# A transformer block on one core: a second annealed instruction order, from a model with another cost for GpSimd's power

## The chip, the cores and the metric

The kernel runs on one core of one Trainium2 chip. Times are device microseconds of one execution. Each kernel ran several times, in turns with the kernel before on the same chip. A few executions have a slightly lower granted TensorE clock (a mean of 0.990 to 0.993 of full speed in place of 0.996 to 1.000). Where a difference under 1 us matters I also give the means of the runs at 0.995 and more, and call them full-clock runs.

## The reference, cut to what matters

One block over 2048 rows of 512: a modulated layer norm, attention of 32 heads over 8 keys each (every second row back), a second modulated layer norm, and a gated feed-forward of width 1792.

```python
mod = (_silu(c) @ w_mod).reshape(...)               # sa, ca, ga, sb, cb, gb
h = _layernorm(x) * (1 + ca) + sa
x = x + ga * _A_ref(h, A_wqkv, A_wo)                # sliding dilated attention
h = _layernorm(x) * (1 + cb) + sb
x = x + gb * _B_ref(h, B_w_gate, B_w_up, B_w_down)  # (gelu(h Wg) * (h Wu)) Wd

def _layernorm(x, axis=-1, eps=1e-05):
    m = jnp.mean(x, axis=axis, keepdims=True)
    v = jnp.var(x, axis=axis, keepdims=True)
    return (x - m) / jnp.sqrt(v + eps)
```

The part the change is named after is the `1 / sqrt(v + eps)`, which GpSimd computes as a power, two columns at a time, 16 times in the kernel.

## The kernel before

The kernel first records 1016 operations, each with an engine, a modelled duration, and what it reads and writes. Then it emits them in the order of one long list, `ORDER`. The list was found outside the kernel, by annealing over the model. Every engine runs its own operations in the order in which they stand, so the list fixes five in-order streams.

```python
ORDER = [
    55, 5, 0, 7, 8, 9, 42, 43, 40, 41, 2, 6, 13, 33, 34, 44, 45, 137, 139, 16, 275, 138, 140, 10, 46, 141, ...
]                                                   # 1016 numbers, cut

def op(self, eng, us, fn, r=(), w=(), pri=0.0, lat=None, table=None, dma=None, after=(), late=0.0, col=0):
    lat = {"pe": 0.2, "act": 0.13, "dve": 0.12, "pool": 0.45, "sp": 0.0}[eng] if lat is None else lat
    ...
def emit(self):
    placed = self.order()                           # asserts that ORDER is a permutation, models the times
    pes, early = [o for o in placed if o.eng == "pe"], True
    for o, q in zip(pes, pes[1:]):
        early = early and o is not self.first       # fillers only before the first projection
        q.fill = max(q.warm, int((q.at - o.at - o.us - 0.1) / 0.216)) if early else 0
    ...
```

The rows are worked on in five groups: two of 256 rows, then three of 512. The operations that the argument touches are these (layer norm, attention's product and fold, the reciprocal of the softmax, the last group's output):

```python
# layer norm, per pair of 128-row blocks; line 522 is the power on GpSimd, line 526 the normalisation on VectorE
gp(0.65, lambda rstd=rstd: nc.gpsimd.tensor_tensor(out=rstd[:], in0=rstd[:], in1=neghalf[:, 0:2],
                                                  op=ALU.pow), r=[rstd, neghalf], w=[rstd], pri=p)
...
# attention: a product of 128x2048 on VectorE (lines 654, 660 with k; 746, 752 with v), then a fold on TensorE
dve(1.14, lambda ...: nc.vector.tensor_tensor(out=t[:], in0=_ap(q...), in1=_ap(k...), op=ALU.mult), ...)
pe(0.22, fold, r=[pq[t], M], w=LT, pri=p, col=1)    # four 32-column matmuls side by side (line 670)
...
ss = T("psB", [P, cn], F32, "ss")                   # PSUM tag psB has two buffers
pe(0.05 + cn * 0.0007, sums, r=[F1, e], w=[ss], pri=p - 1000, col=1)
dve(0.06 + cn * 0.0064, lambda: nc.vector.reciprocal(out=rinv[:], in_=ss[:]), r=[ss], w=[rinv], pri=p)   # line 723
...
x1_ps = T("psB", [P, D], F32, "x1_ps")              # output projection, same tag (line 777)
...
parts = 2 if g == NG - 1 and c4 == n // P - 1 else 1   # the last output block is written in two halves
```

Of the kernel before, what the change touches and what calls it, by code (L numbers as in the profile page):

```python
# [9 lines left out]
ALU = mybir.AluOpType  # L10
# [5 lines left out]
NEG = -1.0e9  # L16

ORDER = [
    55, 5, 0, 7, 8, 9, 42, 43, 40, 41, 2, 6, 13, 33, 34, 44, 45, 137, 139, 16, 275, 138, 140, 10, 46, 141, 35, 36, 37,
    47, 273, 265, 1, 51, 48, 267, 56, 142, 143, 11, 144, 38, 39, 49, 53, 274, 52, 145, 12, 50, 57, 58, 146, 147, 54,  # L20
    59, 148, 150, 60, 266, 62, 268, 276, 277, 269, 149, 61, 278, 280, 270, 14, 66, 271, 64, 28, 159, 279, 272, 67,
    468, 63, 93, 155, 458, 65, 160, 156, 15, 70, 3, 71, 4, 151, 469, 32, 460, 92, 459, 281, 21, 282, 68, 284, 283, 69,
    153, 154, 161, 162, 90, 466, 461, 462, 467, 157, 286, 463, 285, 91, 465, 464, 689, 19, 17, 287, 690, 163, 94, 95,
    288, 96, 97, 158, 164, 307, 98, 291, 99, 24, 308, 77, 78, 292, 72, 470, 171, 687, 471, 100, 472, 289, 152, 295,
    293, 294, 296, 101, 313, 695, 102, 473, 103, 303, 104, 23, 297, 314, 305, 299, 474, 173, 170, 688, 697, 172, 174,
    73, 75, 298, 304, 475, 306, 478, 476, 477, 479, 300, 76, 74, 165, 18, 696, 22, 325, 175, 105, 176, 177, 691, 698,
    106, 107, 108, 692, 290, 694, 326, 309, 310, 301, 109, 178, 302, 311, 312, 110, 693, 699, 113, 486, 487, 20, 488,
    492, 489, 496, 493, 502, 497, 503, 703, 179, 700, 701, 180, 111, 181, 702, 112, 81, 82, 494, 495, 79, 80, 83, 315,
    169, 481, 114, 490, 182, 84, 484, 183, 704, 115, 116, 119, 117, 118, 120, 329, 491, 706, 330, 327, 89, 336, 184,
    707, 185, 482, 123, 333, 124, 186, 480, 187, 121, 122, 500, 504, 334, 328, 125, 708, 705, 485, 335, 483, 501, 713,  # L30
    505, 188, 189, 729, 723, 331, 166, 320, 168, 127, 126, 730, 714, 332, 337, 338, 339, 340, 727, 728, 724, 341, 128,
    129, 29, 167, 192, 130, 26, 131, 322, 193, 190, 191, 323, 342, 498, 499, 711, 725, 726, 721, 722, 712, 132, 731,
    732, 343, 524, 344, 516, 345, 194, 196, 197, 133, 199, 195, 519, 717, 715, 198, 200, 718, 346, 201, 719, 517, 518,
    136, 134, 135, 241, 716, 347, 221, 202, 203, 520, 25, 318, 348, 349, 526, 350, 521, 522, 243, 27, 523, 720, 528,
    242, 244, 223, 232, 245, 231, 351, 204, 206, 233, 527, 234, 352, 222, 511, 525, 353, 224, 225, 205, 235, 317, 319,
    316, 354, 217, 219, 216, 218, 85, 86, 227, 207, 208, 355, 220, 321, 324, 226, 228, 229, 230, 365, 364, 30, 236,
    238, 237, 733, 87, 88, 247, 239, 529, 530, 531, 734, 358, 359, 368, 369, 246, 533, 362, 532, 258, 372, 248, 249,
    31, 251, 259, 252, 240, 709, 253, 209, 356, 210, 211, 213, 212, 367, 366, 357, 360, 370, 371, 214, 373, 250, 534,
    745, 748, 361, 363, 535, 260, 536, 746, 254, 261, 262, 506, 255, 374, 375, 263, 376, 377, 256, 215, 402, 404, 537,
    509, 432, 434, 538, 513, 747, 507, 378, 428, 382, 379, 403, 433, 384, 383, 380, 381, 749, 405, 385, 386, 406, 539,  # L40
    540, 388, 750, 710, 751, 752, 430, 387, 389, 427, 429, 756, 431, 510, 435, 436, 541, 542, 407, 409, 408, 390, 391,
    410, 423, 412, 414, 425, 264, 392, 393, 753, 394, 411, 395, 417, 418, 420, 419, 754, 421, 413, 415, 422, 424, 416,
    543, 437, 444, 426, 755, 544, 445, 438, 454, 508, 446, 439, 447, 396, 735, 740, 512, 545, 514, 397, 399, 400, 257,
    398, 401, 546, 440, 441, 757, 515, 555, 448, 442, 556, 549, 758, 759, 760, 550, 623, 625, 609, 611, 593, 595, 449,
    548, 547, 594, 596, 761, 624, 608, 610, 612, 626, 627, 762, 763, 618, 619, 764, 597, 621, 620, 558, 639, 765, 553,
    641, 638, 640, 642, 453, 622, 643, 633, 635, 559, 560, 551, 645, 557, 563, 552, 554, 644, 766, 634, 767, 646, 603,
    614, 561, 768, 647, 769, 450, 562, 636, 564, 598, 599, 571, 572, 637, 605, 601, 616, 613, 615, 565, 604, 617, 566,
    567, 568, 573, 569, 570, 600, 602, 575, 580, 574, 576, 577, 455, 738, 606, 607, 629, 631, 648, 649, 651, 770, 771,
    659, 650, 582, 744, 451, 578, 457, 628, 579, 452, 630, 632, 456, 661, 739, 652, 654, 653, 655, 656, 443, 658, 675,
    772, 660, 581, 583, 669, 681, 682, 584, 662, 657, 742, 737, 773, 586, 585, 741, 743, 784, 587, 736, 775, 676, 677,  # L50
    678, 679, 774, 588, 591, 589, 590, 683, 663, 684, 664, 685, 665, 686, 680, 776, 785, 787, 670, 666, 671, 592, 882,
    672, 673, 667, 788, 884, 789, 778, 779, 858, 883, 885, 792, 838, 782, 860, 840, 857, 786, 780, 777, 781, 783, 790,
    791, 793, 886, 827, 829, 828, 796, 794, 797, 887, 830, 831, 859, 861, 837, 888, 872, 889, 839, 841, 890, 873, 875,
    874, 868, 833, 832, 852, 800, 891, 795, 802, 804, 803, 870, 798, 799, 835, 876, 834, 836, 854, 805, 801, 823, 825,
    822, 824, 867, 869, 871, 826, 853, 848, 855, 878, 880, 877, 809, 850, 856, 811, 810, 812, 879, 806, 807, 881, 842,
    862, 864, 844, 813, 808, 843, 863, 865, 845, 846, 814, 847, 849, 892, 904, 851, 893, 815, 905, 910, 911, 898, 866,
    912, 906, 907, 894, 895, 913, 816, 668, 674, 817, 818, 899, 900, 901, 908, 909, 896, 897, 902, 914, 819, 820, 821,
    941, 961, 963, 943, 962, 942, 944, 945, 964, 916, 918, 965, 917, 956, 958, 919, 920, 921, 922, 924, 923, 915, 903,
    971, 957, 959, 960, 973, 967, 966, 968, 969, 981, 925, 982, 983, 972, 974, 951, 970, 975, 984, 953, 927, 926, 928,
    929, 930, 985, 952, 954, 955, 937, 939, 932, 931, 933, 946, 936, 934, 938, 940, 935, 948, 977, 979, 976, 978, 947,  # L60
    949, 950, 986, 980, 992, 993, 994, 998, 987, 988, 995, 996, 997, 1010, 989, 990, 991, 1011, 999, 1004, 1005, 1012,
    1006, 1007, 1013, 1008, 1014, 1015, 1000, 1001, 1009, 1002, 1003,
]


# [21 lines left out]
class Plan:  # L87
# [20 lines left out]
        return t  # L108

    def op(self, eng, us, fn, r=(), w=(), pri=0.0, lat=None, table=None, dma=None, after=(), late=0.0, col=0):  # L110
        lat = {"pe": 0.2, "act": 0.13, "dve": 0.12, "pool": 0.45, "sp": 0.0}[eng] if lat is None else lat
        o = Op(eng, us, lat, fn, pri, table, dma)
        norm = lambda a: a if isinstance(a, tuple) else (a, None)
        hit = lambda a, b: a is None or b is None or a == b
        r, w = [norm(a) for a in r], [norm(a) for a in w]
# [99 lines left out]
def kernel(  # L215
# [13 lines left out]
    nc = tc.nc  # L229
# [36 lines left out]
    pe, act, dve, gp, dma = E.pe, E.act, E.dve, E.pool, E.dma  # L266
# [21 lines left out]
    neghalf = ctile([P, 4], F32, "neghalf")  # L288
# [112 lines left out]
    for b in (1, 0):  # L401
        dma(524e3, lambda dq, b=b: dq.dma_start(
            out=wm01[:, :, b * D:(b + 1) * D], in_=w_mod[:, b * D:(b + 1) * D].rearrange("(t p) n -> p t n", p=P)),
            w=[(wm01, b)], pri=-999.5 + 0.5 * (1 - b), bw=340e3)
# [6 lines left out]
    for d4 in range(4):  # L411
        dma(131e3, lambda dq, d4=d4: dq.dma_start(
            out=woP[32 * d4:32 * d4 + 32, :, :],
            in_=bass.AP(A_wo.tensor, A_wo.offset + 4 * D * d4, [[16 * D, H], [D, 4], [1, D]])), w=[(woP, d4)],
            pri=-987, bw=200e3)
# [7 lines left out]
    for i in range(2):  # L423
        lo, hi = i * FT // 2, (i + 1) * FT // 2
        dma(918e3, lambda dq, lo=lo, hi=hi: dq.dma_start(
            out=WdP[:, lo:hi, :], in_=B_w_down[lo * P:hi * P, :].rearrange("(t p) n -> p t n", p=P)),
            w=[(WdP, ft) for ft in range(lo, hi)], pri=-888 + i, bw=335e3, late=1.0)
# [65 lines left out]
    def ln(g, dst, off, p, seq, tags=("psF", "psF"), sums=None):  # L493
        n = GROUPS[g][1]
        xns = []
        for half in range(n // 256):
# [3 lines left out]
            rstd = T("rstd", [P, 2], F32, "rstd", seq)  # L500
            xn = T("xn1" if seq == "ln1" else "xn2", [P, 2, D], BF16, "xn", seq)
            xns.append(xn)
            if sums is not None:
                nm, var = sums[half], mv
                dve(0.09, lambda nm=nm: nc.vector.tensor_scalar_mul(out=nm[:], in0=nm[:], scalar1=-1.0 / D), r=[nm],  # L505
                    w=[nm], pri=p)
                for i in range(2):
                    act(0.75, lambda i=i, xn=xn, nm=nm, mv=mv, c0=c0: nc.scalar.activation(  # L508
                        out=xn[:, i, :], in_=x[g, c0 + i], func=ACT.Square, bias=nm[:, i:i + 1],
                        accum_out=mv[:, 0, i:i + 1]), r=[x.key(g, c0 + i), nm], w=[(mv, i), (xn, i)], pri=p - 1000)  # L510
                dve(0.09, lambda rstd=rstd, mv=mv: nc.vector.tensor_scalar(  # L511
                    out=rstd[:], in0=mv[:, 0, :], scalar1=1.0 / D, scalar2=1e-5, op0=ALU.mult, op1=ALU.add), r=[mv],
                    w=[rstd], pri=p)
            else:
                for i in range(2):
                    dve(0.59, lambda i=i, st=st, c0=c0: nc.vector.bn_stats(out=st[:, i, :], in_=x[g, c0 + i]),  # L516
                        r=[x.key(g, c0 + i)], w=[(st, i)], pri=p)
                    dve(0.09, lambda i=i, st=st, mv=mv: nc.vector.bn_aggr(out=mv[:, i, :], in_=st[:, i, :]), r=[(st, i)],
                        w=[(mv, i)], pri=p)
                dve(0.09, lambda rstd=rstd, mv=mv: nc.vector.tensor_scalar_add(out=rstd[:], in0=mv[:, :, 1],  # L520
                                                                               scalar1=1e-5), r=[mv], w=[rstd], pri=p)
            gp(0.65, lambda rstd=rstd: nc.gpsimd.tensor_tensor(out=rstd[:], in0=rstd[:], in1=neghalf[:, 0:2],  # L522
                                                              op=ALU.pow), r=[rstd, neghalf], w=[rstd], pri=p)
            for i in range(2):
                def norm(i=i, xn=xn, mv=mv, rstd=rstd, c0=c0, nm=sums and sums[half]):
                    nc.vector.tensor_scalar(  # L526
# [4 lines left out]
        if tags is None:  # L531
# [5 lines left out]
            for dt in range(DT):  # L537
# [3 lines left out]
                    r=[(dst, dt), (scl, off), (modT, off)], w=[(dst, dt)], pri=p)  # L541
# [357 lines left out]
```

## Time and profile before

| | before |
|---|---|
| time, median of 3 runs | 245.52 us (245.42 to 245.95) |
| profiled run | 245.00 us, span 243.3 |
| TensorE busy | 235.3 us of the span |
| first QKV matmul starts | 12.14 us |
| last matmul ends | 239.41 us |
| from there to the end of the span | 3.87 us |

Here are three more readings that the result is to be held against. The first is the chain of work that ended last, by engine, in shares of the span:

```profile
PE 70%; DVE 17%; DMA 5%; issue 2%; POOL 2%; ACT 2%; DVEq 0%; ACTq 0%; POOLq 0%
```

Read back from the last instruction, the chain leaves TensorE for 30% of the span: much of it goes through VectorE, and 2% through GpSimd's power. The second is the group of the powers (line, engine, operation, output<-input, count | busy us, mean ns | idle before):

```profile
L522 POOL TENSOR_TENSOR rstd<-rstd,neghalf 128x2 f32<-128x2 f32 x16 | 17.5, 1094 | 162.4 <-DVE rstd L511 140.1
```

Sixteen powers take 1.09 us each on average; the prediction shows that this mixes ones of 0.7 and ones of 1.6 and more. The third is what lies behind the longest of TensorE's waits for VectorE, in the timelines of VectorE and then of TensorE (start, duration, operation, in brackets the idle time and what ended it):

```profile
46.69 1.22 DVE L856 TENSOR_TENSOR woP<-woP,gaB 128x2048 bf16<-128x2048 bf16 x1
47.83 1.22 DVE L654 TENSOR_TENSOR pq<-qT,kT 128x2048 bf16<-128x2048 bf16 x1
48.96 0.55 DVE L723 RECIPROCAL rinv<-ss 128x64 f32<-128x64 f32 x1
```

### The profile page before, as it was taken

To read this page: it belongs to the slowest core of one execution; us is meant where nothing else is said; L and a number is where in the kernel's file an instruction comes from. 1 tells how busy PE (TensorE), PEld (TensorE's weight loads), DVE (VectorE), ACT (ScalarE), POOL (GpSimd) and SP (SyncE) were. 2 spreads that over 40 slices of the span, in tenths; PEclk is the share of its full clock that TensorE was granted. 3 is DMA by queue.
4 is the path that set the end of the run, shared out by engine and by line. 5 is a ranking of instruction groups with operands and counts; after the bars stand their busy time and mean duration, and the time that the engine had idled before them with its cause. 6 is when DMAs were issued, how large, how long until landed. Compare 5 with 4: busy or idle time off the path is not lost.

```text
span 243.3 us, 4304 instructions
## 1 busy us (share of the span) xinstructions
PE 235.3 (97%) x1660; PEld 128.2 (53%) x1680; DVE 163.4 (67%) x317; ACT 148.5 (61%) x278; POOL 25.7 (11%) x45
## 2 busy tenths in 40 slices
PE   7999999999999999999999999999999999999993
PEld 2499555644469645775443444444444444444461
DVE  3878998999999999669985577982422413221222
ACT  2288799678958763894588865328467442665400
POOL 1287212002000300120000011000000100000000
PEclk9999999999999999999999999999999999999999
DMA  5999999898999338269022904210000412000011
GB/s 162 354 316 270 195 195 211 201 238 197 270 285 274 110 94 178 60 180 142 11 65 57 221 9 90 43 43 1 3 0 0 108 26 86 0 0 0 3 43 43
DMA packets 38970, 29.10 MB, mean 120 GB/s; under 512 B 14117, under 2 KB 38054, under 8 KB 38950
## 3 DMA queue, kind: packets, MB, share of 16 engines
q1 hardware_dynamic: 38800, 28.83, 49.8%
q8 instruction: 13, 0.21, 0.4%
q14 instruction: 7, 0.06, 0.1%
q10 hardware_dynamic: 150, 0.00, 0.0%
HBM read 21.40 MB, written 4.28 MB: 106 GB/s over the span
## 4 chain that ended last, share of the span: by engine, by line
PE 70%; DVE 17%; DMA 5%; issue 2%; POOL 2%; ACT 2%; DVEq 0%; ACTq 0%; POOLq 0%
PE y_ps L827 20%; PE u_ps L800 20%; PE g_ps L800 19%; PE x_ps L777 4%; DVE pq L654 4%; DMA wqkv<-in_A_wqkv_dram 3%; DVE pq L660 3%; DVE pv L752 3%; PE o_ps L762 2%; POOL rstd L522 2%; DVE st L516 2%; PE LT L670 2%; PE qkv_ps L603 1%; DVE xn L526 1%; DMA x_sg<-in_A_x_dram 1%
## 5 line engine op out<-in xcount | busy, mean ns | idle before, releaser
L800 PE MATMUL u_ps<-h2T,Wu 128*128 128x512 bf16 (+1 forms) x280 | 54.4, 336 | 0.5 <-ACT gl L809 0.3
L800 PE MATMUL g_ps<-h2T,Wg 128*128 128x512 bf16 (+1 forms) x280 | 54.7, 337 | 0.1
L827 PE MATMUL y_ps<-WdP,hht 128*128 128x512 bf16 (+1 forms) x230 | 49.1, 366 | 0.4
L809 ACT ACTIVATE gl<-g_ps 128x512 bf16<-128x512 f32 x56 | 33.0, 603 | 25.1 <-PE g_ps L800 24.8
L603 PE MATMUL qkv_ps<-hT,wqkv 128*128 128x512 bf16 (+1 forms) x229 | 43.7, 339 | 0.1
L812 DVE TENSOR_TENSOR hht<-gl,ub 128x512 bf16<-128x512 bf16 x56 | 22.6, 422 | 28.8 <-ACT ub L811 20.3
L811 ACT CAST ub<-u_ps 128x512 bf16<-128x512 f32 x56 | 31.7, 589 | 14.9 <-PE u_ps L800 11.7
L800 PEld LDWEIGHTS <-Wg 128*128 128x128 bf16 x280 | 27.0, 98 | 23.0 <-issue 1.5
L800 PEld LDWEIGHTS <-Wu 128*128 128x128 bf16 x280 | 27.0, 98 | 22.7 <-issue 2.0
L827 PEld LDWEIGHTS <-hht 128*128 128x128 bf16 x238 | 23.1, 98 | 24.6 <-issue 0.4
L522 POOL TENSOR_TENSOR rstd<-rstd,neghalf 128x2 f32<-128x2 f32 x16 | 17.5, 1094 | 162.4 <-DVE rstd L511 140.1
L603 PEld LDWEIGHTS <-wqkv 128*128 128x128 bf16 x232 | 24.9, 114 | 13.6 <-issue 1.3
L654 DVE TENSOR_TENSOR pq<-qT,kT 128x2048 bf16<-128x2048 bf16 x24 | 28.8, 1215 | 0.3
L746 DVE TENSOR_TENSOR pv<-e,vR 128x2048 bf16<-128x2048 bf16 x24 | 28.5, 1219 | 0.0
L538 ACT ACTIVATE h2T<-h2T,modT,scl 128x512 bf16<-128x512 bf16 (+1 forms) x20 | 13.2, 726 | 15.1 <-DMA h2T<-xn 15.1
L840 DVE TENSOR_TENSOR ot<-y_ps,x_sg 128x512 bf16<-128x512 f32 (+1 forms) x13 | 8.2, 648 | 18.5 <-PE y_ps L827 18.5
L781 DVE SCALAR_TENSOR_TENSOR x_sg<-x_ps,x_sg 128x512 bf16<-128x512 f32 x16 | 11.0, 687 | 14.2 <-PE x_ps L777 7.2
L777 PE MATMUL x_ps<-woP,oT 128*128 128x512 bf16 x57 | 14.9, 379 | 0.7 <-DVE rinv L723 0.5
L508 ACT ACTIVATE xn<-x_sg,xsum 128x512 bf16<-128x512 bf16 x16 | 11.5, 721 | 4.3 <-DVE xsum L505 4.3
L516 DVE BATCH_NORM_STATS2 st<-x_sg 128x6 f32<-128x512 bf16 x16 | 10.6, 679 | 3.3 <-DMA x_sg<-in_A_x_dram 3.3
L619 ACT CAST kT<-qkv_ps 128x512 bf16<-128x512 f32 x16 | 9.5, 602 | 1.8 <-PE qkv_ps L603 1.8
L619 ACT CAST qT<-qkv_ps 128x512 bf16<-128x512 f32 x16 | 9.5, 600 | 1.3 <-PE qkv_ps L603 1.3
(93 smaller groups left out, 201.2 us busy)
## 6 DMA issues: line engine op xcount, KB each, us to landing
vR<-scr SPq DMA_DIRECT2D x24, 260.0 KB, 5.0
wm<-in_w_mod_dram SPq DMA_DIRECT2D x6, 512.0 KB, 6.7
vR<-scr SPq DMA_DIRECT2D x8, 264.0 KB, 5.2
out_dram<-ot SPq DMA_DIRECT2D x15, 128.0 KB, 1.8
Wg<-in_B_w_gate_dram SPq DMA_DIRECT2D x2, 896.0 KB, 11.0
Wu<-in_B_w_up_dram SPq DMA_DIRECT2D x2, 896.0 KB, 5.4
WdP<-in_B_w_down_dram SPq DMA_DIRECT2D x2, 896.0 KB, 12.6
scr<-vT SPq DMA_DIRECT2D x6, 264.0 KB, 2.4
```

The costliest lines, as they stand in the source:

```text
L516: dve(0.59, lambda i=i, st=st, c0=c0: nc.vector.bn_stats(out=st[:, i, :], in_=x[g, c0 + i]), r=[x.key(g, c0 + i)], w=[(st, i)], pri=p)
L522: gp(0.65, lambda rstd=rstd: nc.gpsimd.tensor_tensor(out=rstd[:], in0=rstd[:], in1=neghalf[:, 0:2], op=ALU.pow), r=[rstd, neghalf], w=[rst ...
L603: nc.tensor.matmul(ps[:, j - j0, :], lhsT=wqkv[b][:, dt, j:D:4], rhs=h_cols(hT, g, dt), start=(dt == 0), stop=(dt == DT - 1))
L619: act(0.475, lambda t=t, off=off, j0=j0, ps=ps: nc.scalar.copy(out=t[:, j0:j0 + nj, off:off + n], in_=ps[:]), r=[ps], w=[(t, j) for j in r ...
L654: dve(1.14, lambda j=j, wg=wg, t=pq[m]: nc.vector.tensor_tensor(out=t[:], in0=_ap(q[g][:, j, 0:n], [[0, 4], [1, n]]), in1=_ap(k[g][:, j, : ...
L746: dve(1.14, lambda jj=jj, jl=jl, wg=wg, t=pv[m]: nc.vector.tensor_tensor(out=t[:], in0=_ap(e[:, wg, :], [[0, 4], [1, n]]), in1=vR[g][jj][: ...
L777: nc.tensor.matmul(x1_ps[:], lhsT=oT[:, j, c4 * P:(c4 + 1) * P], rhs=woP[:, j, :], start=(j == 0), stop=(j == 3))
L800: nc.tensor.matmul(ps[:, ft - f0, :], lhsT=Wt[ft // 7][:, dt, ft % 7 * P:(ft % 7 + 1) * P], rhs=h_cols(h2, g, dt), start=(dt == 0), stop=( ...
L809: act(0.485, lambda gl=gl, ps=gu[0]: nc.scalar.activation(out=gl[:], in_=ps[:], func=ACT.Gelu_apprx_tanh), r=[gu[0]], w=[gl], pri=p, table ...
L811: act(0.475, lambda ub=ub, ps=gu[1]: nc.scalar.copy(out=ub[:], in_=ps[:]), r=[gu[1]], w=[ub], pri=p)
L812: dve(0.335, lambda gl=gl, ub=ub, ht=ht: nc.vector.tensor_tensor(out=ht[:], in0=gl[:], in1=ub[:], op=ALU.mult), r=[gl, ub], w=[ht], pri=p)
L827: nc.tensor.matmul(y_ps[:], lhsT=hh[ft // nf][:, ft % nf, c4 * P:(c4 + 1) * P], rhs=WdP[:, ft, c0:c0 + w], start=(ft == 0), stop=(ft == FT ...
```

## The change

The intent: in the model's terms the power costs 0.65 us and 0.45 us of latency wherever it stands. In the new model it costs 0.7 and 0.07, and it waits for VectorE's products of two inputs. The order was annealed again over that model. The new constants stand in the program too, three of them: 0.65 becomes 0.7, the power's latency becomes 0.07, and the latency of GpSimd's other operations falls from 0.45 to 0.15. What differs in the kernel's text is that and the order:

```diff
 ORDER = [
-    55, 5, 0, 7, 8, 9, 42, 43, 40, 41, 2, 6, 13, 33, 34, 44, 45, 137, 139, 16, 275, 138, 140, 10, 46, 141, 35, 36, 37,
+    1, 56, 55, 0, 4, 7, 5, 6, 8, 13, 137, 139, 9, 42, 138, 140, 43, 40, 41, 44, 141, 142, 16, 275, 265, 10, 33, 34,
     ... (every line of the list differs: another permutation of the same 1016 numbers)
 ]
@@
-        lat = {"pe": 0.2, "act": 0.13, "dve": 0.12, "pool": 0.45, "sp": 0.0}[eng] if lat is None else lat
+        lat = {"pe": 0.2, "act": 0.13, "dve": 0.12, "pool": 0.15, "sp": 0.0}[eng] if lat is None else lat
@@
-            gp(0.65, lambda rstd=rstd: nc.gpsimd.tensor_tensor(out=rstd[:], in0=rstd[:], in1=neghalf[:, 0:2],
-                                                              op=ALU.pow), r=[rstd, neghalf], w=[rstd], pri=p)
+            gp(0.7, lambda rstd=rstd: nc.gpsimd.tensor_tensor(out=rstd[:], in0=rstd[:], in1=neghalf[:, 0:2],
+                                                              op=ALU.pow), r=[rstd, neghalf], w=[rstd], pri=p, lat=0.07)
```

In words, the new order loads rows 2-3 ahead of rows 0-1, moves GpSimd's constants ahead of the first power, starts the attention of the first group earlier, moves loads of gate and up weights, enters the folding layout of TensorE 16 times in place of 14, and ends on a 128x256 output piece in place of a 128x512 one.

## The prediction

> **What bounds the kernel now.** I read the page's first two sections, then the PE's waits, then the timelines of PE, DVE and POOL, and last the times of landing.
>
> Page, busy time and the 40 slices:
>
> ```profile
> PE 235.3 (97%) x1660; PEld 128.2 (53%) x1680; DVE 163.4 (67%) x317; ACT 148.5 (61%) x278; POOL 25.7 (11%) x45
> PE   7999999999999999999999999999999999999993
> DVE  3878998999999999669985577982422413221222
> PEclk9999999999999999999999999999999999999999
> ```
>
> TensorE has work in every slice, at full clock. VectorE is its equal only from slice 3 to about 17 (18 to 105 us); after that it idles. A busy PE may still hide gaps, so I looked at its waits (engine, line, releaser: us, times, longest):
>
> ```profile
> PE x_ps L777 <- DVE rinv L723: 0.5, 1, 0.5
> PE LT L700 <- DVE m L695: 0.4, 1, 0.4
> PE u_ps L800 <- ACT gl L809: 0.3, 1, 0.3
> ```
>
> These are nearly all its waits after the first projection: 1.2 us. To check it against work: a 512-column matmul starts every 0.216 us in the trace. After the first projection there are 448 of gate and up (96.8 us), 224 of down (48.4), 192 of QKV (41.5), 64 of output projection (13.8), each counted as 512 columns, and 64 rounds of four folds side by side (13.8). Small matmuls (transposes, max, broadcast, modulation) are some 7 us. Sum 221. They take from 12.14 us to the end of the last matmul at 239.25, 227.1 us. So at most 6 us are lost between, and a new order can win only from these 6, from the 12.14 ahead and from the 4 us tail.
>
> Two kinds of loss are visible in the PE timeline (start, us):
>
> ```profile
> 12.14 0.84 PE L607 MATMUL qkv_ps<-hT,wqkv 128*128 128x256 bf16 x6
> 55.08 1.48 PE L670 MATMUL LT<-pq,Mph 128*32 128x512 bf16 x24
> 56.49 5.37 PE L603 MATMUL qkv_ps<-hT,wqkv 128*128 128x512 bf16 x24
> ```
>
> The first row is the first projection. The next two: 24 folds are 6 rounds, 1.30 us, but the next group starts 1.41 after the first fold, so leaving the folding layout costs 0.11.
>
> What the change is about is GpSimd's power (1/sqrt of two variances), seen in POOL's timeline and VectorE's waits:
>
> ```profile
> 35.17 0.71 POOL L522 TENSOR_TENSOR rstd<-rstd,neghalf 128x2 f32<-128x2 f32 x1 [7.85 <-DVE mv L518]
> 38.72 1.79 POOL L522 TENSOR_TENSOR rstd<-rstd,neghalf 128x2 f32<-128x2 f32 x1 [2.85 <-DVE rstd L520]
> ...
> 56.48 1.62 POOL L522 TENSOR_TENSOR rstd<-rstd,neghalf 128x2 f32<-128x2 f32 x1 [15.96 <-DVE rstd L511]
> ```
>
> ```profile
> DVE xn L526 <- POOL rstd L522: 3.3, 6, 0.7
> ```
>
> The same power takes 0.7 us or 1.6 to 1.8. At 38.72 and 56.48 VectorE has just begun a 1.2 us product (38.55 and 56.32 in its timeline); at 35.17 it runs a reciprocal and small operations. The delay costs VectorE 3.3 us of idling in six places, not TensorE.
>
> **What the Trainium skill says.** "SBUF — State Buffer", section "Who interferes with whom": a VectorE instruction with two SBUF inputs contends with a GpSimd instruction that reads SBUF, and the one that issues later waits for the whole of the other. The trace agrees: 0.69 to 0.79 us alone, 1.5 to 1.86 behind a product, about one product more. "Perfetto Trace Analysis", section "Identifying the Most-Contended Engine" (with the overview's remark that matmul busy time is a bad metric): hence my count of starts above; here count and busy time agree to 6 us.
>
> **The change part by part.** The computation, tiles and buffers stay. The constants of the model (0.7 and 0.07 us for the power in place of 0.65 and 0.45) reach the chip only through the order and through the number of filler matmuls before the first projection. I numbered the operations as the kernel creates them and compared the two lists engine by engine.
>
> (1) The start. Before: rows 0-1 load first, and VectorE does their statistics and normalisation before the rest. After: rows 2-3 load first; VectorE does eight row statistics before it finishes the first hT column that the projection reads, as before, but three small aggregations and two additions more (5 x 0.09 = 0.45 us), and the first group's normalisation comes after the statistics of rows 4-7. Walking it with this trace: first landing 3.86, second 4.54; four statistics at 0.62 to 0.64 and six small ones bring VectorE to 7.15; rows 4-7 land at 7.61; four statistics to 10.1; normalisations of both groups with small ones between, to 12.1; hT to 12.45. On TensorE both transposes of the second group (0.22 each) and three fillers (0.65) now stand before the first projection: 12.15 + 0.45 + 0.65 = 13.3. Before, its four parts ended at 13.27, with one transpose between; now at 13.3 + 0.87 = 14.15. **+0.9 us**, on the path because TensorE is full from there. The QKV weights land at 12.1 in both orders (same transfers ahead), so they no longer bind. The value weights land at 16.71; the first value block now stands fourth, at 14.15 + 3 x 0.87 = 16.75: no gap to speak of.
>
> (2) GpSimd. The selection constants move from 16-21.5 us to before the first power; they end by about 5 us, before its input exists at 7.15. Powers after: in the first five pairs the next normalisation is at least 1.2 us of other VectorE work away or no large product starts behind the power; for group 0's second layer norm a multiply by a PSUM operand stands where a product stood. Of the 2.7 us of idling before 75 us I expect about 0.9 to remain, so VectorE gains **1.8 us** in its full stretch.
>
> (3) What TensorE gets of that. For every fold, max or broadcast I added up VectorE's work before its producer and TensorE's work before it. The largest lead that VectorE needs is 6.4 us before and 7.6 after (fourth fold of group 0; then 7.1 at its broadcast). TensorE starts 0.9 later and VectorE idles 1.8 less, so the need is just met: I expect the two waits near 49 and 66 us to go (**-0.8**), and no large new one.
>
> (4) Layout changes: 14 stretches of folds and sums before, 16 after: 2 x 0.11 = **+0.2**.
>
> (5) The tail. Before, the last piece is a 128x512 one (0.69 us eviction, 128 KB out); after, a 128x256 one (0.38, 64 KB, which land 0.2 faster by the table of transfers): **-0.4**.
>
> (6) Transfers. Gate and up weights move to about 44 us (before: gate at 13.35, landing 23.69), half of the down weights goes ahead of the shuffled values of group 2. These landed at 77.67 before, as their product began (77.70). After, I reckon the half needed first at about 70 against a need at 77, the other at 78 against 85. Slack, but the thinnest I found. **0**.
>
> Sum: +0.9 - 0.8 + 0.2 - 0.4 = -0.1, so 245.4. An annealed order should also recover a little of the 2 to 3 us of loss that I could not attribute; I take 0.3 for it: **245.1 us**.
>
> **The rivals.** (a) GpSimd's waits are on the path. For it: the chain of work that ended last gives POOL 2% (some 5 us), and its blocked powers at 22.33, 38.72 and 56.48 are in it. Then undoing them gives back one product each where VectorE is full, about 2.5 us, and the shifted start is repaid by the earlier attention of group 0 (its max is subtracted after 12.4 us of TensorE work in place of 16.3): 242.5 to 243.5. Against it: TensorE waited only 0.9 us for VectorE in all, and a chain can run through work that ends just in time. (b) The start and the higher lead bite: if VectorE falls 1 to 2 us further behind (its landing or QKV copies late), TensorE waits at folds of group 0, and the sum becomes 247 to 248. For it: a lead of 7.6 with no margin. Against it: it is one place, with projection blocks right behind it. (c) The weight transfers collide with the shuffled values, and products of group 2 wait: +2 to +4 us, 247.5 to 249.5. For it: half of the down weights (0.9 MB, some 4 us at the 200 to 280 GB/s of those slices) goes ahead. Against it: 7 us of slack.
>
> **Range and chances.** Central 245.1; (a) and (b) are about equally likely, (c) less. I take 243.0 to 247.6. Two per cent is 4.9 us. Faster by that needs 240.6, which would use up nearly all of the 6 us lost plus something of the start, while the start seems to get later: 0.03. Slower by that needs (b) and (c) together, or a gap that I did not see: 0.06. Within: 0.91.
>
> **What would show it.** Step 1: the first qkv matmul at about 13.3, not 12.1. Step 2: powers of 0.7 us with at most a few over 1.5, and VectorE's wait for POOL clearly under 3.3. Step 3: PE waits of DVE under 1 us, and none before 30 us over 0.5. Step 4: about the same PE busy time, within 1 us. Step 5: the last eviction 128x256. Step 6: no DVE wait for the shuffled values. If the time falls by more than 2 us with a later start, my reading that TensorE's gaps are few is wrong; if it rises by more than 2, look at VectorE between 18 and 30 us, then at transfers between 60 and 80.

## More of the kernel before

```profile
49.57 1.02 PE L777 MATMUL x_ps<-woP,oT 128*128 128x512 bf16 x4 [0.46 <-DVE rinv L723]
```

The output projection needs a PSUM buffer. The buffer is free when VectorE has read the sums out of it, and in VectorE's order two products stand ahead of that reciprocal. So a short operation, late behind long ones, holds up the engine that sets the pace.

## The result, and the profile after

| | before | after |
|---|---|---|
| median of 4 runs, same chip | 245.47 us (245.25 to 245.95) | 243.99 us (243.76 to 244.47) |
| ratio | 1 | 0.994 (95%: 0.9919 to 0.9961) |
| span of the profiled run | 243.3 | 242.8 (its time of 244.47 is the slowest of the four) |
| first QKV matmul starts | 12.14 | 13.27 |
| last matmul ends | 239.41 | 239.31 |
| from there to the end | 3.87 | 3.45 |

A ratio is the mean time of one kernel's fast runs over the mean of the other's fast runs of the same rounds, so it is not quite the ratio of the medians. The change gained 0.6%, 1.5 us by the means, which counts as the same at a threshold of 2%.

TensorE's waits after the change (engine, line, releaser: us, times, longest), and the chain that ended last:

```profile
PE warm_ps L435 <- DVE neghalf L306: 1.3, 1, 1.3
PE qkv_ps L603 <- DMA wqkv<-in_A_wqkv_dram: 0.5, 1, 0.5
PE y_ps L827 <- issue: 0.2, 1, 0.2
```

```profile
PE 91%; DMA 5%; SPq 1%; issue 1%; ACT 0%; ACTq 0%; DVE 0%
```

The first wait lies before the start and is in both kernels. The three waits for VectorE and ScalarE that the prediction showed are gone. From 17.4 us on, where TensorE waits for the value weights to land, the chain does not leave TensorE again: 91% in place of 70%, and VectorE and GpSimd are out of it. The last 0.2 us are no loss: a 512-column matmul starts every 0.216 us, the page of this kernel counts 238 weight loads of line 827 and 229 matmuls, so some records are missing, and a gap of one such step is one of them.

The start, in TensorE's timeline:

```profile
12.62 0.81 PE L440 MATMUL warm_ps<-warm 128*128 128x512 bf16 x3
13.27 1.04 PE L607 MATMUL qkv_ps<-hT,wqkv 128*128 128x256 bf16 x8
14.14 2.78 PE L603 MATMUL qkv_ps<-hT,wqkv 128*128 128x256 bf16 x24
17.43 0.73 PE L603 MATMUL qkv_ps<-hT,wqkv 128*128 128x256 bf16 x5 [0.51 <-DMA wqkv<-in_A_wqkv_dram]
```

Three fillers and the first projection lie where the prediction put them, and from 14.14 on the blocks follow without a gap. The one at 17.43 is the value weights: they landed at 17.39 here, against 16.71 in the profile before.

The reciprocal that TensorE waited for at 49 us before, in VectorE's timeline after:

```profile
47.29 0.55 DVE L723 RECIPROCAL rinv<-ss 128x64 f32<-128x64 f32 x1
47.76 1.16 DVE L856 TENSOR_TENSOR woP<-woP,gaB 128x2048 bf16<-128x2048 bf16 x1
48.83 2.35 DVE L654 TENSOR_TENSOR pq<-qT,kT 128x2048 bf16<-128x2048 bf16 x2
```

It now stands ahead of both products and is done by 47.84 in place of 49.51.

GpSimd's two longest powers before 75 us, VectorE's products at the first of them, and VectorE's wait for GpSimd in all:

```profile
27.56 2.73 POOL L522 TENSOR_TENSOR rstd<-rstd,neghalf 128x2 f32<-128x2 f32 x1 [0.69 <-DVE rstd L520]
39.39 1.60 POOL L522 TENSOR_TENSOR rstd<-rstd,neghalf 128x2 f32<-128x2 f32 x1 [9.10 <-DVE rstd L520]
```

```profile
27.40 2.34 DVE L660 TENSOR_TENSOR pq<-qT,kT 128x2048 bf16<-128x2048 bf16 x2
```

```profile
DVE xn L526 <- POOL rstd L522: 3.4, 7, 0.9
```

Six powers took over 1.5 us before, three do now (the third, 2.19, at 104.27). The one at 27.56 began 0.16 us behind two products that ran back to back, and ended 0.55 us after the second. But VectorE's wait in total did not fall: 3.4 us against 3.3. It moved. Place by place in the trace, it was 2.72 us before 75 us and is 0.64 now; the rest is at 103, 106 and after 140 us, where VectorE idles anyway.

The end, in VectorE's timeline, before and then after:

```profile
239.45 0.69 DVE L840 TENSOR_TENSOR ot<-y_ps,x_sg 128x512 bf16<-128x512 f32 x1 [0.76 <-PE y_ps L827]
```

```profile
239.35 0.42 DVE L840 TENSOR_TENSOR ot<-y_ps,x_sg 128x256 bf16<-128x256 f32 x1 [0.40 <-PE y_ps L827]
```

The span thus divides into three parts: up to the first QKV matmul (+1.13), from there to the last matmul's end (227.27 before, 226.05 after: -1.22), and the tail (-0.42). The sum is -0.5, less than the 1.5 of the times, because the two profiles are of unlike runs: this one of the slowest of its four (244.47), the one before of a run (245.00) faster than all four of its kernel. The first experiment's profile is of a run (243.36) near its kernel's median.

### The profile page after: what moved, and what is told of

It is laid out like the page before. It is cut to its first block, busy times and chain, and to the rows that moved or that the text cites. A ratio compares the mean times of both kernels' runs of the same rounds, so it can differ in the third digit from the quotient of the medians.

```text
span 242.8 us, 4313 instructions
## 1 busy us (share of the span) xinstructions
PE 236.5 (97%) x1667; PEld 129.0 (53%) x1685; DVE 164.5 (68%) x317; ACT 149.6 (62%) x278; POOL 21.5 (9%) x45
## 4 chain that ended last, share of the span: by engine, by line
PE 91%; DMA 5%; SPq 1%; issue 1%; ACT 0%; ACTq 0%; DVE 0%
PE u_ps L800 20%; PE y_ps L827 20%; PE g_ps L800 20%; PE qkv_ps L603 16%; PE x_ps L777 6%; DMA wqkv<-in_A_wqkv_dram 4%; PE o_ps L762 3%; PE LT L670 3%; DMA touched<-in_w_mod_dram 1%; PE rB L731 1%; SPq L372 1%; SPq L384 1%; PE LT L700 0%; PE tp L550 0%; PE ss L719 0%
## 5 line engine op out<-in xcount | busy, mean ns | idle before, releaser
L827 PE MATMUL y_ps<-WdP,hht 128*128 128x512 bf16 (+1 forms) x229 | 49.9, 366 | 0.6 <-issue 0.2
L522 POOL TENSOR_TENSOR rstd<-rstd,neghalf 128x2 f32<-128x2 f32 x16 | 15.7, 983 | 171.8 <-DVE rstd L511 146.4
L654 DVE TENSOR_TENSOR pq<-qT,kT 128x2048 bf16<-128x2048 bf16 x24 | 28.3, 1219 | 0.2
L538 ACT ACTIVATE h2T<-h2T,modT,scl 128x512 bf16<-128x512 bf16 (+1 forms) x20 | 13.3, 723 | 11.2 <-DMA h2T<-xn 11.2
L777 PE MATMUL x_ps<-woP,oT 128*128 128x512 bf16 x60 | 15.4, 379 | 0.2
L768 ACT CAST oT<-o_ps 128x512 bf16<-128x512 f32 x16 | 9.2, 597 | 7.5 <-PE o_ps L762 7.5
L619 ACT CAST vT<-qkv_ps 128x512 bf16<-128x512 f32 x16 | 9.3, 590 | 2.5 <-PE qkv_ps L603 2.4
```

The source lines that it names most:

```text
L522: gp(0.7, lambda rstd=rstd: nc.gpsimd.tensor_tensor(out=rstd[:], in0=rstd[:], in1=neghalf[:, 0:2], op=ALU.pow), r=[rstd, neghalf], w=[rstd ...
L538: act(0.29 + n * 0.0008, lambda dt=dt: nc.scalar.activation(out=dst[:, 0:n // P, dt, :], in_=dst[:, 0:n // P, dt, :], func=ACT.Identity, s ...
L654: dve(1.14, lambda j=j, wg=wg, t=pq[m]: nc.vector.tensor_tensor(out=t[:], in0=_ap(q[g][:, j, 0:n], [[0, 4], [1, n]]), in1=_ap(k[g][:, j, : ...
L777: nc.tensor.matmul(x1_ps[:], lhsT=oT[:, j, c4 * P:(c4 + 1) * P], rhs=woP[:, j, :], start=(j == 0), stop=(j == 3))
L827: nc.tensor.matmul(y_ps[:], lhsT=hh[ft // nf][:, ft % nf, c4 * P:(c4 + 1) * P], rhs=WdP[:, ft, c0:c0 + w], start=(ft == 0), stop=(ft == FT ...
```

## The experiments

The theory, A below: TensorE is the bound; the changed order pays 0.7 to 1.1 us for a later start, gains in the middle because VectorE reaches the operations that TensorE waits for in time, and gains 0.4 in the tail. The first rival: GpSimd's powers sit on the path directly, so their waits come off the time one for one. A second rival takes the later start for a pure loss that could be had back. A further one came up on the way: the old order's up weights land late in some runs (D in the later texts). There were three sessions on three chips, each with its own runs of the kernel before.

One question needed no run. The constants alone, with the old order, build to instruction streams that are identical on all five engines (and the new order alone builds to those of the changed kernel). So the constants act through the order only.

### The changed kernel again

Edit: none.

> The changed kernel once more, as the yardstick of this chip. Known from before: 0.994 of the kernel before (243.99 against 245.47 us). Both theories expect 0.993 to 0.996. In its profile the first qkv matmul again at 13.2 to 13.3 us and one TensorE wait of up to 0.7 us at 17 us for the value weights' landing; a run in which they land before 16.9 us should have no such wait and a span of some 242.2 in place of 242.8.

Measured: 243.47 us (243.36 to 244.19), ratio 0.9938 (0.9912 to 0.9965), span 241.6. The start in TensorE's timeline:

```profile
12.84 1.06 PE L607 MATMUL qkv_ps<-hT,wqkv 128*128 128x256 bf16 x8
13.73 4.53 PE L603 MATMUL qkv_ps<-hT,wqkv 128*128 128x256 bf16 x40
```

The result repeats. In the view of TensorE's waits not one is left between the first projection and the end but the missing record at line 827, and the value weights came in time: 40 matmuls without a gap. Against the profile before, the start is +0.70, the middle 225.37 against 227.27 (-1.90), the tail -0.43: -1.6 in all. Matmul by matmul, the middles of the two profiles of the changed kernel differ in one place alone, by 0.65 us at the wait for value weights. So that wait comes with the run's transfers and is no fixed cost of the order.

### The changed order with the old start

The first 72 operations of the changed order, put in the old sequence.

```diff
-ORDER = AFTER
+ORDER = sorted(AFTER[:72], key=BEFORE.index) + AFTER[72:]
```

> The changed order, but its first 72 operations in the relative order they had before (rows 0-1 loaded and normalised first). Theory A (a tight VectorE): the first qkv matmul comes back to about 12.2 us, but TensorE then waits as much longer for VectorE's first products near 20 to 22 us, so the time is within 0.4 us of the changed kernel (ratio to before 0.993 to 0.996). Rival B (the late start is a plain cost that the rest repays): the whole 0.9 to 1.1 us is saved, 243.0 us, ratio 0.990.

Measured: 243.55 us (243.03 to 244.90), ratio 0.9938 (0.9908 to 0.9969; by full-clock runs -1.73 us against -1.48): the same as the changed kernel within the noise, though the first projection starts at 11.70, 1.1 earlier than in the run above. TensorE's waits:

```profile
PE qkv_ps L603 <- DMA wqkv<-in_A_wqkv_dram: 0.4, 2, 0.2
PE LT L670 <- DVE pq L660: 0.4, 1, 0.4
```

By the distances between starts, against the same matmuls in the run above, the three gaps are 0.39 (13.2), 0.38 (16.2) and 0.56 us (21.93): 1.33 together, and a transpose that stood ahead of the first projection now stands behind it (0.23). The earlier start is spent waiting for the key and value weights and then for a product of VectorE. So the later start shows no cost of its own here: weights and VectorE did not follow an earlier one. The rival that saw 0.7 to 1.1 us to be had at the start falls.

### The old order with the new start

```diff
-ORDER = BEFORE
+ORDER = sorted(BEFORE[:72], key=AFTER.index) + BEFORE[72:]
```

(The same with 81 operations would not build: it broke the order in which PSUM buffers are handed out.)

> The order of before, but its first 72 operations in the relative order of the changed kernel. Theory A: TensorE starts about 1 us later, but its two waits for VectorE near 49 and 66 us (0.9 together) shrink, so 245.3 to 245.9 us, ratio 0.999 to 1.002. Rival B: the later start is paid in full, 246.4 to 246.6, ratio 1.004. If the start were where the gain comes from, it would be below 0.998.

Measured: 245.65 us (244.94 to 246.0), ratio 1.0011 (0.9983 to 1.004); first projection at 12.80.

```profile
PE u_ps L800 <- DMA Wu<-in_B_w_up_dram: 0.6, 1, 0.6
PE LT L700 <- DVE m L695: 0.4, 1, 0.4
PE x_ps L777 <- DVE rinv L723: 0.3, 1, 0.3
```

The new start gives nothing, and both waits for VectorE stay. There is also a wait that I had not looked for: the up weights, issued at 60 us in this order, came 0.6 us late at 72 us.

### The old order with the new tail

```diff
-ORDER = BEFORE
+ORDER = BEFORE[:911] + sorted(BEFORE[911:], key=AFTER.index)
```

> The order of before with only its last 105 operations (the last row group's gate, up, down and stores) in the order of the changed kernel. My step 5: the last eviction becomes 128x256 in place of 128x512 and the last transfer 64 KB: 0.3 to 0.5 us saved, 245.0 to 245.2 us, ratio 0.998. Rival (the end of the span does not depend on it): 1.000.

Measured: 244.5 us (243.94 to 246.16), ratio 0.9979 (0.9946 to 1.0012). By the medians the tail is worth 0.45 us, by the profile 0.44 (3.43 against 3.87); the interval includes 1, so the profile has to carry it. The run profiled was the slowest, and shows why:

```profile
PE u_ps L800 <- DMA Wu<-in_B_w_up_dram: 2.3, 1, 2.3
```

At a granted clock of 0.997, so not for the clock's sake, TensorE waited 2.3 us for up weights at 72.9.

### No power on GpSimd, old order and changed order

The power becomes a 128x2 multiply on VectorE (0.15 to 0.16 us each in the trace). The result is wrong; the comparison with the reference is too loose to see a layer norm's scale here, and neither is a version to keep. The power itself on VectorE doesn't compile, so the honest form was not to be had.

```diff
-gp(0.65, lambda rstd=rstd: nc.gpsimd.tensor_tensor(out=rstd[:], in0=rstd[:], in1=neghalf[:, 0:2], op=ALU.pow), ...)
+dve(0.09, lambda rstd=rstd: nc.vector.tensor_tensor(out=rstd[:], in0=rstd[:], in1=neghalf[:, 0:2], op=ALU.mult), ...)
```

> Wrong result on purpose: the order of before, with each power on GpSimd replaced by a multiply of the same 128x2 tile on VectorE, so that no VectorE instruction waits for GpSimd. Theory A (the powers cost VectorE, and TensorE only where it waits for VectorE): VectorE's 2.7 us of waiting before 75 us go, TensorE's two waits of 0.4 us near 49 and 66 us go with them, nothing more: 244.0 to 244.4 us, ratio 0.995 to 0.998. Rival B (blocked powers lie on the path, one product each): 2.5 us, ratio 0.990. Rival C (the powers do not matter at all for the end): 1.000.

> Wrong result on purpose: the same replacement in the changed order. Theory A: TensorE has no wait for VectorE left in that order, so nothing is gained: 0.993 to 0.995 of the kernel before, as the changed kernel has itself (0.9938). Rival B: one to three more products of 1.1 us gone, 0.985 to 0.990.

Measured, old order: 243.32 us (243.09 to 244.06), ratio 0.9914 (0.988 to 0.9948). Changed order: 243.61 us (243.4 to 243.92), ratio 0.992 (0.9888 to 0.9952). By its ratio the first lies near rival B's 0.990 and outside A's range. But it is further from 1 than the times suggest, because three of the eleven runs of the kernel before had a clock of 0.990 here. By full-clock runs the old order gains 1.58 us and the changed one 1.44, against the 1.48 that the changed kernel gained in both of its own sessions.

Part of that is not the middle. In these two profiles the last records of GpSimd's program show 0.07 us from its final clearing of semaphores to the end of its drain, against 0.54 and 0.55 in the profiles with powers. This 0.47 us shows in the tail: 2.96 us in the changed order without powers against 3.43 with, and 3.40 against 3.87 in the old one. It is not the powers' doing: the next experiment runs 32 of them and has the short drain and the tail of 2.96 too. Taking it off, the powers' waits were worth 1.58 - 0.47 = 1.1 us in the old order. The profile's middle says 227.27 - 226.04 = 1.23, and matmul by matmul all of it comes from two places: TensorE's waits at 49.6 and 66.0 us are gone, worth 0.62 and 0.61. In the changed order nothing is gained in the middle (225.35 against 225.37). Its time doesn't show the shorter tail either: its first projection started at 13.47 us, 0.63 later than in the first experiment; why, no run here shows. The wait of TensorE that is left in the old order without powers, besides the one before the start:

```profile
PE u_ps L800 <- ACT gl L809: 0.3, 1, 0.3
```

The two waits for VectorE are gone without a change of order. Here is the first of them in TensorE's timeline, before and then without powers:

```profile
48.09 1.03 PE L777 MATMUL x_ps<-woP,oT 128*128 128x512 bf16 x3
49.57 1.02 PE L777 MATMUL x_ps<-woP,oT 128*128 128x512 bf16 x4 [0.46 <-DVE rinv L723]
```

```profile
47.88 1.89 PE L777 MATMUL x_ps<-woP,oT 128*128 128x512 bf16 x7
```

The view gives an idle time of 0.46 us, counted from the modelled end of the matmul ahead, 0.38 after its start. But without a wait the next one starts 0.216 after it, so the wait cost 0.835 - 0.216 = 0.62. In VectorE's timeline of the run without powers the reciprocal still stands behind both products, but comes 1.14 us earlier (0.94 counted from the first projection, which starts 0.20 earlier in this run):

```profile
46.69 1.22 DVE L654 TENSOR_TENSOR pq<-qT,kT 128x2048 bf16<-128x2048 bf16 x1
47.82 0.55 DVE L723 RECIPROCAL rinv<-ss 128x64 f32<-128x64 f32 x1
```

So there are two ways to take away the same wait: free VectorE of its idling (here), or put the short operation first (the changed order). This is the middle ground between the theory and the first rival: GpSimd's waits did reach TensorE, through VectorE, but for 1.2 us of the 2.7 that VectorE idled, not one for one.

### Every power twice, changed order

```diff
-            gp(0.7, lambda rstd=rstd: nc.gpsimd.tensor_tensor(out=rstd[:], ...), r=[rstd, neghalf], ...)
+            gp(0.7, lambda rstd=rstd: twice(rstd), r=[rstd, neghalf], ...)
+    def twice(rstd):                                  # the first goes to a spare tile
+        for to in (spare, rstd):
+            nc.gpsimd.tensor_tensor(out=to[:], in0=rstd[:], in1=neghalf[:, 0:2], op=ALU.pow)
```

> The changed order with every power run twice on GpSimd (the first into a spare tile), so 16 more of 0.7 us or more. Theory A: VectorE waits longer for GpSimd (3.3 us become 8 or more), its slack of some tenths in the first 75 us is used up, and TensorE begins to wait for it: 0.3 to 1.5 us slower than the changed kernel, ratio 0.995 to 1.000. Rival (VectorE's waits for GpSimd are all absorbed): no change, 0.9938. Rival B (on the path): 16 x 0.7 in part, over 3 us slower, above 1.005.

Measured: 246.67 us (246.25 to 246.96), ratio 1.0041 (1.0008 to 1.0074), which is 2.5 us over the changed kernel (1.0041 - 0.9938 = 0.0103 of 245.3), 3.0 by full-clock runs: above what A gave, and below or at the edge of what the rival gave. VectorE's wait for GpSimd, and TensorE's longest waits (lines are 5 further down in this kernel, 25 less for the power):

```profile
DVE xn L531 <- POOL rstd L497: 11.2, 11, 1.8
```

```profile
PE LT L705 <- DVE m L700: 0.7, 1, 0.7
PE g_ps L805 <- ACT h2T L543: 0.5, 1, 0.5
```

VectorE idles 7.8 us more for GpSimd. TensorE's waits add up to some 2 us in the view, but the middle is 3.2 us longer than in the first experiment (228.58 against 225.37), lost in places from 22 to 206 us; the times rose less because of the tail that is 0.47 shorter. The order that needs no relief from VectorE has no room for a further delay of it either. A was too small here by 1 us and more: I took the slack for larger than it is. By size the rival's "over 3 us" fits as well; what speaks against one for one is that 3.2 of the 7.8 us reached TensorE.

### The up weights earlier, old order

The two loads of up weights, which stood well behind a layer-norm transpose on the queue, are moved: one ahead of it, one right behind it.

```diff
-ORDER = BEFORE
+ORDER = move(move(BEFORE, [25], before=132), [27], after=132)   # 25, 27: load Wu; 132: transpose to h2T
```

> The order of before, with only the two loads of the up weights moved ahead in the queue (the first ahead of the first layer norm's transpose, the second right behind it). In two profiles of the last session TensorE waited 0.6 and 2.3 us at 72 us for the second of these to land, in the recorded profile of before it did not. Theory D (part of the gain is that the changed order has these weights early): the slow runs of before (246.2 to 246.5) go away, the median falls by 0.2 to 0.5, ratio 0.996 to 0.999. Rival (those waits are noise of the single profile): 1.000, with the same scatter.

Measured: 246.48 us (246.24 to 248.75; that one at a clock of 0.990), ratio 1.0051 (1.0006 to 1.0097): slower, a miss. No wait for up weights shows; a longer one is there (TensorE's waits, then ScalarE's timeline):

```profile
PE x_ps L777 <- ACT oT L768: 1.9, 1, 1.9
```

```profile
65.26 0.60 ACT L538 ACTIVATE h2T<-h2T,modT,scl 128x256 bf16<-128x256 bf16 x1 [2.37 <-issue]
65.76 1.05 ACT L768 CAST oT<-o_ps 128x512 bf16<-128x512 f32 x2
```

The transposed rows landed later (at 65.2 us, though issued at 59.2 in place of 58.9), with the first half of the weights ahead of them on the queue, and ScalarE, which runs in order, held the evictions to oT behind the copy of h2T (65.26 against 62.52 before). The experiment bred its own wait and says nothing on what the landing of up weights costs the old order.

### The first up block first, old order

In the first group's feed-forward, blocks that use the second half of the up weights trade places with blocks that use the first half, which is loaded first.

```diff
-ORDER = BEFORE
+ORDER = swap(swap(BEFORE, [241..245], [221..225]), [231..235], [216..220])   # five operations a block
```

> The order of before, but in the first row group's gate and up the blocks that read the first half of the up weights trade places with those that read the second half, so the second half is needed some 3 us later; no transfer moves. Theory D (in the slow runs of before TensorE waits at 72 us for that half to land): runs of 246.2 to 246.9 are gone, the others stay, mean ratio 0.997 to 0.999. Rival (the slow runs have another cause): they stay, ratio 1.000.

Measured: 245.22 us (244.32 to 246.40), ratio 0.998 (0.9942 to 1.0019): inconclusive. Its one long run had a clock of 0.990. The clock also explains most long runs of the kernel before in these sessions (246.38 at 0.990, 247.9 at 0.993, 246.72 to 246.88 at 0.990). Three are left at full clock: 246.46, 246.20 and 246.24, of 28, and the 246.16 above. Of 26 full-clock runs with the changed middle none lies over 0.75 us above its kernel's median. That fits late up weights in the old order alone, but only the 246.16 has a trace that shows it, so their share of the gain stays open.

### The value blocks later, changed order

One more key block ahead of the first value block, against the wait for value weights.

```diff
-ORDER = AFTER
+ORDER = move(AFTER, [161, 162], before=70)   # a QKV block and its eviction, ahead of the first value block
```

> The changed order with one key block of the second group moved ahead of the two value blocks of the first. Expected: TensorE's wait of up to 0.7 us at 17 us for the value weights goes in the runs that have it: median 0 to 0.3 us below the changed kernel, ratio 0.992 to 0.9938, unless the copies of keys and values that follow on ScalarE start VectorE's first products later, then 0.995.

Measured: 243.74 us (243.45 to 244.40), ratio 0.992 (0.9885 to 0.9954; by full-clock runs -1.59 us against -1.48). No wait of TensorE at the start, middle 225.35, first projection at 13.4. This is the changed kernel's own time within the noise: the wait in the recorded profile is rare, or small.

### Both: the old start, relieved

The old start in the changed order, with the block above moved, and two row statistics of VectorE moved behind the product that TensorE waited for.

```diff
-ORDER = AFTER
+o = sorted(AFTER[:72], key=BEFORE.index) + AFTER[72:]
+ORDER = move(move(o, [161, 162], before=70), [460, 687], after=93)
```

> The try for a faster version: the changed order with the start as before (first qkv matmul at 11.7 us), the key block ahead of the value blocks, and two row statistics (0.64 us each) moved behind the fourth first-group product, because TensorE waited there. Theory A (each tenth that VectorE is relieved of before that product is a tenth for TensorE, as long as no other lead binds): the waits at 16 and 22 us go, 0.5 to 0.8 us below the changed kernel, ratio 0.990 to 0.992. Rival (the next leads bind at once): as the changed kernel, 0.9938.

Measured: 243.42 us (242.78 to 244.79), ratio 0.9909 (0.9868 to 0.9951), span 241.7, first projection at 12.26. One wait is left before the end (0.2 in the view, 0.37 between starts):

```profile
PE qkv_ps L603 <- DMA wqkv<-in_A_wqkv_dram: 0.2, 1, 0.2
```

It has the lowest mean of all (by full-clock runs -2.12 us against -1.48), but its interval covers that of the changed kernel, so it is not shown to be faster.

### The changed order with its first 446 operations in the old sequence

```diff
-ORDER = AFTER
+ORDER = sorted(AFTER[:446], key=BEFORE.index) + AFTER[446:]
```

> The changed order, with its first 446 operations (to about 70 us) in the relative order they had before. Theory A (most of the gain is VectorE's time won before 70 us): little of the gain is left, only the tail's 0.3 to 0.4 and the 0.6 of waits at 105 and 108 us: 244.0 to 244.6 us, ratio 0.996 to 0.998. Rival (the gain is made in the later part): 0.993 to 0.995.

Measured: 245.72 us (244.58 to 247.01), ratio 0.9995 (0.9953 to 1.0036), span 244.0: the gain is gone. TensorE's waits and timeline:

```profile
PE g_ps L800 <- ACT ub L811: 1.3, 1, 1.3
...
PE x_ps L777 <- DVE rinv L723: 0.5, 1, 0.5
PE LT L700 <- DVE m L695: 0.4, 1, 0.4
```

The two waits of the old order are back at 49.7 and 66.1 us, and those at 105 and 108 are not. The 1.3 us at 87 (1.47 between starts) I take for an artefact of the seam between the two orders, so the 1.5 us lost are not all the first part's, and the time alone does not decide between theory and rival. What the profile shows is that the two waits for VectorE belong to the order of the first 70 us.

## Why the prediction was right or wrong

The time was right: 244.0 against 245.1, in the range of 243.0 to 247.6, and within 2%. Its middle value was 1.1 us too high: it forecast 0.4 us less than before, and 1.5 came. The term that was mis-sized is what TensorE gets in the middle of the kernel (step 3). By its own steps:

1. **The start, +0.9.** Right: first projection at 13.27 (predicted 13.3), 12.84 in the repeated run, where transfers came earlier. What I missed is that a later start is not a loss of that size: the old start in the changed order begins 1.1 us earlier and loses 1.3 to waits. "No gap to speak of" for the value weights was wrong in the recorded run (0.67 us between starts) and right in the next (none).
2. **GpSimd, 2.7 us of idling down to 0.9 before 75 us.** Right in the place that counts (0.64), wrong as a sign in the whole: I wrote that the wait for GpSimd would be clearly under 3.3, and it is 3.4. The order moved the waits to where VectorE has time.
3. **What TensorE gets, -0.8.** The mechanism was right, the size too small. Both waits went, but they were worth 0.62 and 0.61 us by the distance between starts, not the 0.8 together that I took from the view. The reading "1.2 us" of all waits was low for the same reason. Beyond them the waits for ScalarE and PSUM buffers at 105.1 (0.44) and 107.9 (0.23) and a gap of 0.12 at 32.6 went too: 2.0 us in all. Removing the powers from the old order shows that GpSimd's share is 1.2, not 0.8 and not the first rival's 2.5. My 0.3 for losses that I could not attribute was the place where the ScalarE ones belonged; the wait at 105 us stood in the very list of waits that I showed.
4. **Layout changes, +0.2.** Too small: from the matmul ahead of each stretch to the one behind it, the stretches take 0.43 us more together (a missing record on either side taken off). I charged 0.11 for leaving the folding layout and nothing for entering it; in the trace entering costs about 0.09 and leaving 0.10.
5. **The tail, -0.4.** Right: -0.42 in the profile, 0.44 with the tail alone.
6. **Transfers, 0.** No wait for the shuffled values came, as predicted. What I did not see is that the old order has a thin place of its own: up weights 0.6 and 2.3 us late in two profiled runs that kept it.

The repeated run's middle is 1.90 us shorter. Losses gone (-2.0), a transpose moved ahead of the first projection (-0.22), the half-width last matmul (-0.11) and the layout (+0.43) make -1.9, so nothing of size is left over. One sentence of the prediction compares unlike things: its count of work, 221 us, differs by 6 from the 227.1 us that passed; from the busy time of that stretch (224.9) it differs by 4.

Of the rivals, (a), the powers on the path, was right in kind and twice too large; (b), a lead without margin, didn't strike, but its ground was real, as the doubled power and the old start show; (c), colliding transfers, did not occur.

## What to carry to other kernels

When one engine is full, the place of a wait matters more than its length: the total wait of VectorE for GpSimd did not change, and the time fell because it no longer reached TensorE. A short operation that frees a buffer for the full engine belongs ahead of long ones on its in-order engine, and an earlier start is worth only what transfers and the second-busiest engine can follow. Look at a wait's cause in a second run before you mend it: here one of 0.5 us was gone in the next run, and one of 2.3 us showed only in another. And size a wait by the distance between starts: TensorE's waits of 0.46 in the view cost 0.62.

## What the Trainium skill lacked or had wrong

- "SBUF — State Buffer", section "Who interferes with whom": its rule that a VectorE product with two SBUF inputs blocks GpSimd's read for the whole instruction agrees (0.69 us alone, 1.60 behind one product of 1.22). It says nothing of products back to back: here one power waited for two of them and took 2.73 us (2.34 of products). Nor does any page that I looked up give the cost of a 128x2 power on GpSimd, 0.69 us.
- "TensorEngine Tiling (Array Packing)", section "Key Properties": it says that changing the tiling mode drains TensorE, without a cost. The traces show about 0.09 us on entering the four-column layout and 0.10 on leaving it (0.31 between starts in place of 0.216, both ways).
- No page that I looked up has it: from GpSimd's final clearing of semaphores to the end of its last drain, eleven of the fourteen profiles show 0.54 to 0.56 us and three 0.07, and the span ends as much earlier in these. It does not go with the powers: the three are the two kernels without any and the one with every power twice. In the eleven an 8 KB transfer on an instruction queue follows 0.3 to 0.6 us after the end of the span, in the three none does; the cause is not shown.
- No page that I looked up has it: a granted clock of 0.990 to 0.993 as the mean of a run, in place of 0.996 to 1.000, goes with 1.0 to 2.5 us more of 245.
